# Linear attention and gated convolution on one core: the order list behind its first 215 entries is laid out anew

## The chip, the cores and the metric

One core of a Trainium2 chip runs one launch of the kernel. The metric is the device time of that launch in microseconds, here as the median of several runs. Five engines work side by side, each through its own instructions in order: TensorE (PE, with its weight loads shown as PEld), VectorE (DVE), ScalarE (ACT), GpSimd (POOL) and SyncE (SP). Transfers are issued by the queues of POOL, SP and ACT.

## The reference

Eight batches, eight heads, 576 rows, head width 64. The first part is a linear attention with a norm over each head, the second a feed-forward part with a three-tap convolution as its gate.

```python
kv = np.einsum('bhsd,bhse->bhde', k, v)
out = np.einsum('bhsd,bhde->bhse', q, kv)
x = out / sqrt(mean(out * out, -1) + 1e-06) * g_norm     # heads side by side: 8 x 576 x 512
h = np.maximum(x @ w_in, 0.0)                            # 512 -> 1024
gate = sigmoid(conv of h along the rows, 3 taps for each of 1024 columns)
y = (h * gate) @ w_out                                   # 1024 -> 512
```

## The kernel before

The kernel is a set of small operations, each a Python function of a few instructions, and one long list of entries, ORDER (L59 to L135), that says in which order they are issued. An entry is the operation's name, its arguments, and behind an @ the slots that its results take. The loop at L779 issues them one by one, and the lines from L786 chain each engine's instructions in that order. So nothing is moved by the compiler, and the list alone sets the order on each engine. The engines meet where one needs what another has made, or where a slot has to be given up first.

The slots of most matmul results are the eight banks of PSUM. An entry such as `hm.4.0@0` takes banks 0 and 1 (`bank2`), `hs` and `om` take one (`bank`). The next entry that names the same bank waits until all readers of the old result are done. Rings in SBUF work the same way: qT, sq, o32, x, h, tap, kvb, row.

For batch b the entries are, in the order of the data:

- `Lq`, `Lk`, `Lv` (POOL, L347): loads of q, k, v, converted to bf16.
- `kv` or `kz` (PE, L402, L479): k transposed times v for two pairs of heads, 72 small matmuls; `kvd` or `kva` copies the result to kvb on DVE (L414) or ACT (L416). `kx` (SP, L489) makes a copy with the halves of the partitions exchanged.
- `qt` (PE, L433) transposes q, `qd` (DVE, L443) copies it; for batches 6 and 7 a transposing transfer does this, `tq` (SP, L467).
- `ot` or `ox` (PE, L460, L500): q times kv, four small matmuls, for half of the rows (s) and half of the heads (u). `sq` (ACT, L509) squares the result.
- Batches up to 3: `on` (PE, L528) sums the squares over each head, `nl` (ACT, L545) takes the reciprocal root, `mo` (DVE, L556) multiplies into x. Batches 4 to 7, two at a time: `oc` (ACT, L521) copies the result out of PSUM, `ss` (PE, L566) sums, `ln` (ACT, L574) takes the root, `sl` (DVE, L581 to L584) splits it into two parts, `sp` (PE, L593) spreads it and `mu` (DVE, L599) multiplies into x.
- `hk`, `hs`, `hm` (PE, L658, L628, L613): x times 128 columns f of w_in. `rh` or `re` (ACT, L640, L619) is the maximum with zero into h.
- `ta`, `aa`, `ab` (DVE, L681, L682, L687, L692): the taps, two columns of f in one of two tap buffers. `sg` (ACT, L698): the sigmoid. `mg` (DVE, L722): the product with h.
- `om.p.m.0.4` and `om.p.m.4.4` (PE, L732): first and second half of 128 rows m of a pair p of batches times w_out; `oh` (L757) does half of the columns of one block. `ea`, `eh` (ACT, L738, L767) or `ed` (DVE, L743) copy the bank to a row buffer; `st`, `sh` (SP, L748, L777) store it.

ACT holds one set of function tables at a time. The roots (`nl`, `ln`) and the sigmoid (`sg`, `sc`) need different sets, and `act_table` (L224) issues a load when the next operation needs the other one.

Some of the code, cut:

```python
def bank2():
    at = slots.pop(0)
    return banks[:, at:at + 2, :]
...
def hm(b, f):
    ps = T["hm", b, f] = bank2()
    for t in range(NT):
        for s in range(2):
            nc.tensor.matmul(ps[:, s, :HS], w_in_sb[:, t, f * P:(f + 1) * P], T["x", b][:, t, c0:c1], ...)
...
for token in ORDER.split():
    what, _, at = token.partition("@")
    slots[:] = [int(s) for s in at.split(",")] if at else []
    name, *args = what.split(".")
    ops[name](*(int(a) if a.isdigit() else a for a in args))
```

Of the kernel before, what the change touches and what calls it, by code (L numbers as in the profile page):

```python
# [87 lines left out]
rh.2.5.0 on.3.0.1@4 nl.3.0.1@3 aa.1.1.2 mo.3.1.1@0 hs.2.2.1@2 rh.2.2.1 hs.2.0.0@3 rh.2.0.0 ot.3.0.0@0 sq.3.0.0@6
mo.3.0.1 qt.4.0.0@4 qd.4.0.0@3 ta.1.1.3 ab.1.1.2 aa.1.1.1 ot.3.1.0@2 sq.3.1.0@7 hs.2.3.1@6 rh.2.3.1 on.3.0.0@4
nl.3.0.0@4 hs.3.4.1@7 rh.3.4.1 hs.3.1.1@6 rh.3.1.1 on.3.1.0@4 nl.3.1.0@5 mo.3.0.0 hs.3.6.1@7 rh.3.6.1 hs.2.6.0@6  # L90
mo.3.1.0 qt.5.0.0@4 qd.5.0.0@0 ab.1.1.1 qt.4.1.0@0 qd.4.1.0@4 sg.1.1.5 sg.1.1.4 Lq.6.0.4@0 mg.1.1.2 ta.1.1.6@1
ta.1.1.7 aa.1.1.3 hs.2.3.0@7 rh.2.3.0 hs.3.0.1@2 rh.3.0.1 rh.2.6.0 sg.1.1.3 sg.1.1.2 hs.3.7.0@3 hs.3.2.0@4 rh.3.2.0
hs.3.3.0@5 rh.3.3.0 rh.3.7.0 kv.4.0.2@0 kvd.4.0.2@1 hs.3.0.0@2 hs.3.3.1@6 mg.1.1.1 Lk.5.0.4@0 rh.3.3.1 hs.3.2.1@7
rh.3.2.1 hs.3.7.1@4 rh.3.7.1 hs.3.6.0@5 rh.3.6.0 rh.3.0.0 ab.1.1.3 ta.2.2.2@0 ta.2.2.3 hs.3.4.0@3 rh.3.4.0 sg.1.1.7
hs.3.1.0@4 hs.3.5.0@5 sg.1.1.6 rh.3.1.0 qt.5.1.0@0 qd.5.1.0@2 ot.4.0.0@6 sq.4.0.0@0 mg.1.1.3 rh.3.5.0 om.0.7.0.4@2
Lv.5.0.4@1 Lq.7.0.4@1 Lk.6.0.4@1 oc.4.0.0@6 hs.2.7.1@3 rh.2.7.1 ot.4.0.1@0 sq.4.0.1@1 oc.4.0.1@7 kv.5.0.2@4 ta.2.2.0@1
kvd.5.0.2@2 ot.4.1.0@6 oc.4.1.0@8 om.0.7.4.4 aa.2.2.1 ta.2.2.1 ed.0.7@4 aa.2.2.0 ot.5.0.0@4 sq.4.1.0@2 sq.5.0.0@3
# [727 lines left out]
```

## Time and profile before

| | |
|---|---|
| runs | 177.69, 177.53, 177.68 us, median 177.68 |
| the profiled execution | span 175.6 us from its first to its last instruction; its own time isn't given, and what lies around the span is 2.1 us against the median |
| instructions | 5070, of which 2097 are matmuls on PE with a record |
| PE, DVE, ACT, POOL busy | 167.9, 149.5, 148.9, 22.2 us |
| transfers | 29.1 MB, mean 166 GB/s |
| granted clock of PE | 1.00 throughout |

Times in the profile are in microseconds from the first instruction, unless ns is written. L732 is line 732 of the kernel, and a busy time is the union of an engine's instructions. Matmuls overlap: the row of one 512-column matmul lasts 379 ns, while in a row of many they follow each other much more closely. ACT's and DVE's rows overlap a little as well, so what one of them costs is read from start to start. "Idle before" is the engine's idle time ahead of the rows, with what ended it.

### The profile page before, as it was taken

To read this page: it belongs to the slowest core of one execution; us is meant where nothing else is said; L and a number is where in the kernel's file an instruction comes from. 1 tells how busy PE (TensorE), PEld (TensorE's weight loads), DVE (VectorE), ACT (ScalarE), POOL (GpSimd) and SP (SyncE) were. 2 spreads that over 40 slices of the span, in tenths; PEclk is the share of its full clock that TensorE was granted. 3 is DMA by queue.
4 is the path that set the end of the run, shared out by engine and by line. 5 is a ranking of instruction groups with operands and counts; after the bars stand their busy time and mean duration, and the time that the engine had idled before them with its cause. 6 is when DMAs were issued, how large, how long until landed. Compare 5 with 4: busy or idle time off the path is not lost.

```text
span 175.6 us, 5070 instructions
## 1 busy us (share of the span) xinstructions
PE 167.9 (96%) x2097; PEld 100.0 (57%) x2114; DVE 149.5 (85%) x290; ACT 148.9 (85%) x268; POOL 22.2 (13%) x35
## 2 busy tenths in 40 slices
...
GB/s 159 392 323 207 207 207 207 208 208 209 207 241 230 227 207 207 170 182 197 258 181 161 14 134 0 119 123 0 119 63 0 0 0 116 13 239 175 179 304 237
DMA packets 25911, 29.11 MB, mean 166 GB/s; under 512 B 6036, under 2 KB 20384, under 8 KB 25888
## 3 DMA queue, kind: packets, MB, share of 16 engines
...
q10 hardware_dynamic: 544, 1.18, 1.7%
q8 instruction: 16, 0.26, 0.6%
...
## 4 chain that ended last, share of the span: by engine, by line
PE 76%; DVE 12%; ACT 5%; DMA 3%; issue 3%; ACTq 0%; DVEq 0%
PE banks L732 32%; PE banks L628 14%; PE banks L613 9%; PE banks L658 4%; DMA stg<-in_v_dram 3%; PE banks L460 3%; DVE h L722 2%; PE banks L708 2%; ACT taps L698 2%; PE banks L402 2%; PE banks L593 2%; PE banks L433 1%; PE banks L528 1%; DVE taps L681 1%; PE banks L286 1%
## 5 line engine op out<-in xcount | busy, mean ns | idle before, releaser
L732 PE MATMUL banks<-w_out_sb,h 128*128 128x512 bf16 x267 | 62.8, 379 | 1.2 <-issue 0.6
L698 ACT ACTIVATE taps<-taps,cw 128x576 bf16<-128x576 bf16 (+1 forms) x44 | 40.6, 958 | 5.7 <-DVE taps L692 5.5
L732 PEld LDWEIGHTS <-h 128*128 128x128 bf16 x280 | 26.2, 98 | 30.0 <-issue 1.1
L628 PE MATMUL banks<-x,w_in_sb 128*128 128x288 bf16 (+2 forms) x256 | 34.2, 286 | 0.0
L640 ACT ACTIVATE h<-banks 128x288 bf16<-128x288 f32 (+2 forms) x80 | 29.5, 460 | 0.3 <-PE banks L658 0.2
L628 PEld LDWEIGHTS <-w_in_sb 128*128 128x128 bf16 x256 | 24.4, 98 | 7.8 <-issue 0.8
L722 DVE TENSOR_TENSOR h<-h,taps 128x1152 bf16<-128x1152 bf16 (+1 forms) x24 | 22.8, 952 | 1.2 <-ACT taps L698 1.2
L687 DVE TENSOR_TENSOR taps<-taps 128x1152 bf16<-128x1152 bf16 (+1 forms) x22 | 21.5, 978 | 0.5
L509 ACT ACTIVATE sq<-banks 128x576 bf16<-128x576 f32 (+2 forms) x32 | 20.8, 691 | 1.1 <-PE banks L460 1.1
L692 DVE TENSOR_TENSOR taps<-taps,h 128x1152 bf16<-128x1152 bf16 (+1 forms) x22 | 21.4, 972 | 0.3
L681 DVE TENSOR_SCALAR taps<-h,cw 128x576 bf16<-128x576 bf16 (+1 forms) x44 | 18.7, 424 | 0.6 <-ACT h L665 0.5
L682 DVE TENSOR_SCALAR taps<-h,cw 128x576 bf16<-128x576 bf16 (+1 forms) x44 | 18.4, 418 | 0.0
L738 ACT ACTIVATE row<-banks 128x512 f32<-128x512 f32 x23 | 13.5, 597 | 5.7 <-PE banks L732 4.2
L658 PE MATMUL banks<-x,w_in_sb 128*128 128x288 bf16 (+2 forms) x128 | 17.7, 286 | 0.1
L613 PE MATMUL banks<-x,w_in_sb 128*128 128x288 bf16 x128 | 16.9, 286 | 0.0
L556 DVE SCALAR_TENSOR_TENSOR x<-banks,cw,rs 128x576 bf16<-128x576 f32 (+2 forms) x16 | 13.0, 816 | 3.9 <-ACT rs L545 3.6
L658 PEld LDWEIGHTS <-w_in_sb 128*128 128x128 bf16 x128 | 12.0, 98 | 4.4 <-issue 0.5
L227 ACT ACT_TABLE_LOAD x10 | 12.8, 1283 | 2.0 <-issue 1.8
L613 PEld LDWEIGHTS <-w_in_sb 128*128 128x128 bf16 x128 | 12.3, 98 | 3.7 <-issue 0.2
L443 DVE COPY qT<-banks 128x1152 bf16<-128x1152 bf16 (+2 forms) x13 | 8.8, 681 | 5.7 <-PE banks L433 5.7
L545 ACT ACTIVATE rs<-banks,eps_sb 128x576 f32<-128x576 f32 (+2 forms) x16 | 11.8, 740 | 1.1 <-PE banks L528 1.1
L599 DVE SCALAR_TENSOR_TENSOR x<-o,cw,banks 128x576 bf16<-128x576 f32 (+2 forms) x16 | 12.1, 810 | 0.7 <-PE banks L593 0.5
...
## 6 DMA issues: line engine op xcount, KB each, us to landing
out_dram<-row SPq DMA_DIRECT2D x35, 256.0 KB, 2.3
...
```

What stands on the lines that cost most here:

```text
L509: nc.scalar.activation(T["sq", b, u, s], T["o", b, u, s], AX.Square)
L613: nc.tensor.matmul(ps[:, s, :HS], w_in_sb[:, t, f * P:(f + 1) * P], T["x", b][:, t, c0:c1], start=(t == 0), stop=(t == NT - 1))
L628: nc.tensor.matmul(ps, w_in_sb[:, t, f * P:(f + 1) * P], T["x", b][:, t, c0:c1], start=(t == 0), stop=(t == NT - 1))
L640: nc.scalar.activation(h, fr, AX.Relu)
L658: nc.tensor.matmul(T[at], w_in_sb[:, t, f * P:(f + 1) * P], T["x", b][:, t, c0:c1], start=(t == 0), stop=(t == NT - 1))
L681: nc.vector.tensor_scalar_mul(tap[:, 0, f % 2, :n, 8:8 + S], h[:, f], cw[:, f:f + 1])
L682: nc.vector.tensor_scalar_mul(tap[:, 1, f % 2, :n, :S], h[:, f], cw[:, 2 * NF + f:2 * NF + f + 1])
L687: nc.vector.tensor_add(tap[:, 1, :, :n, :S], tap[:, 0, :, :n, 7:7 + S], tap[:, 1, :, :n, 1:1 + S])
L692: nc.vector.tensor_add(y, y, span(b, n)[:, 2 * j:2 * j + 2])
L698: nc.scalar.activation(y, y, AX.Sigmoid, scale=cw[:, NF + f:NF + f + 1])
L722: nc.vector.tensor_mul(h, h, tap_of(b, j)[:, 1, :, :n, :S])
L732: nc.tensor.matmul(T["om", p, m], h[:, f, m * P:(m + 1) * P], w_out_sb[:, f, :], start=(f == 0), stop=(f == NF - 1))
```

## The change

The list has 852 entries before and after. The first 215 are the same; the 637 behind them are in a new order with new slots. The multiset of operations is the same but for eight copies that change engine: ed.0.1, ea.0.4, ea.1.8, kvd.3.0.2, ed.2.8, ed.3.0, ed.3.7 and ea.3.6 become ea.0.1, ed.0.4, ed.1.8, kva.3.0.2, ea.2.8, ea.3.0, ea.3.7 and ed.3.6. No function changes. The diff replaces all of the list's lines from L79 on; these are the stretches that matter below, old and new.

```diff
-om.0.2.0.4@5 kv.2.0.2@6 mg.0.1.3 om.0.1.4.4 ab.1.1.0 sg.1.1.0 sg.1.1.1 kvd.2.0.2@2 ot.2.0.1@0 sq.2.0.1@0 ed.0.1@0
-st.0.1 qt.3.1.0@6 qd.3.1.0@1 Lk.4.0.4@1 Lv.4.0.4@0 Lq.5.0.4@2 om.0.2.4.4 on.2.0.1@2 qt.3.0.0@6 qd.3.0.0@2 nl.2.0.1@8
-mo.2.0.1@2 om.0.3.0.4@4 ea.0.2@1 ot.2.1.1@6 ot.2.1.0@2 mg.1.1.0 om.0.3.4.4 ed.0.3@2 sq.2.1.0@1 sq.2.1.1@2 on.2.1.0@0
...
+om.0.1.0.4@2 om.0.2.0.4@5 kv.2.0.2@6 ab.1.1.0 om.0.1.4.4 Lk.4.0.4@1 Lv.4.0.4@0 sg.1.1.0 kvd.2.0.2@0 sg.1.1.1
+qt.3.1.0@0 ot.2.0.1@6 Lq.6.0.4@2 om.0.2.4.4 ta.1.1.5@1 ea.0.1@0 qt.3.0.0@2 Lq.5.0.4@0 qd.3.1.0@1 pn qd.3.0.0@2
+sq.2.0.1@0 on.2.0.1@0 nl.2.0.1@0 om.0.3.0.4@4 ot.2.1.1@0 mo.2.0.1@0 ot.2.1.0@2 ea.0.2@1 sq.2.1.0@0 mg.1.1.0 sq.2.1.1@1
+om.0.3.4.4 ed.0.3@2 on.2.1.0@6 om.0.0.0.4@5 nl.2.1.0@0 on.2.1.1@6 nl.2.1.1@1 hk.1.3.0.0@4 om.0.0.4.4 ta.1.1.2@0
+mo.2.1.0 ot.2.0.0@2 hk.1.3.0.1 mo.2.1.1 hs.2.0.1@0 sq.2.0.0@0 rh.1.3.0 ed.0.0@3 on.2.0.0@6 hs.2.5.1@1 rh.2.0.1@1
+nl.2.0.0@0 rh.2.5.1 kv.3.0.2@4 qt.4.0.0@6 ta.1.1.4 aa.1.1.2 mo.2.0.0 qd.4.0.0@0 ta.1.1.3 ab.1.1.2 aa.1.1.1 ab.1.1.1
+kva.3.0.2@0 ot.3.1.1@0 sq.3.1.1@0 ot.3.0.1@4 sq.3.0.1@1 hs.2.1.1@2 hs.2.4.0@3 hs.2.4.1@6 rh.2.4.0 rh.2.1.1 hs.2.1.0@7
...
+ta.2.2.0@0 ta.2.2.1 mg.1.1.3 rh.3.7.1 rh.3.4.0 rh.3.5.0 rh.3.6.0 om.0.7.0.4@0 ot.4.0.0@2 sq.4.0.0@0 oc.4.0.0@0
+ta.2.2.2@1 aa.2.2.0 ot.4.0.1@4 ot.4.1.0@6 hs.2.7.1@1 tq.6.0@3 st.0.2 st.0.1 st.0.0 sq.4.0.1@1 oc.4.0.1@1 sq.4.1.0@2
+oc.4.1.0@2 rh.2.7.1 kv.5.0.2@2 kvd.5.0.2@1 om.0.7.4.4 ta.2.2.3 ot.5.0.0@2 qt.5.1.0@4 ot.5.0.1@6 ed.0.7@0 om.0.8.0.4@1
...
-om.0.6.4.4 ea.0.6@3 sp.4.0.0.4@6 mu.4.0.0 sp.4.0.1.4@0 hs.2.6.1@5 rh.2.6.1 hs.3.5.1@2 rh.3.5.1 ox.6.0.0@6 sq.6.0.0@0
-oc.6.0.0@4 mu.4.0.1 sp.5.1.1.4@4 mu.5.1.1@2 sg.2.2.3 sp.5.1.0.4@2 mu.5.1.0 hm.4.7@0 sp.5.0.1.4@4 sp.5.0.0.4@6 mu.5.0.1
-mu.5.0.0 hm.4.1@2 re.4.7@0 sg.2.2.1 re.4.1 hm.4.0@4 sg.2.2.0 hm.4.4@0 re.4.4 hm.4.6@6 re.4.6 re.4.0 hm.5.1@2 re.5.1
-mg.2.2.1 hm.5.3@0 re.5.3 tq.7.0@0 st.0.6 ox.6.1.1@6 oc.6.1.1@5 sq.6.1.1@1 ox.6.1.0@4 oc.6.1.0@1 ta.2.2.4@0 ta.2.2.5
...
+om.0.6.4.4 kvd.6.0.2@0 mu.5.1.1@1 sp.4.1.0.4@0 sp.4.0.1.4@6 hs.2.6.1@4 ea.0.6@5 mu.4.1.1 ox.6.0.0@2 rh.2.6.1 mu.4.1.0
+mu.4.0.1 sp.5.1.0.4@0 sp.5.0.1.4@4 Lk.7.0.4@0 Lv.7.0.4@1 st.0.4 hm.4.7@6 mu.5.1.0 mu.5.0.1 oc.6.0.0@0 sg.2.2.0
+sq.6.0.0@0 hm.4.0@0 hm.4.4@2 re.4.7@0 mg.2.2.0 st.0.8 sg.2.2.3 kx.6@0 tq.6.1@0 re.4.0 re.4.4 ox.6.1.1@0 sp.5.0.0.4@4
+hm.4.6@6 re.4.6 mu.5.0.0 hm.5.4@4 re.5.4 hm.5.5@2 sq.6.1.1@1 oc.6.1.1@1 re.5.5 ta.2.2.4@0 ta.2.2.5 hm.4.5@6 kz.7.0.2@0
+mg.2.2.1 hm.4.1@2 aa.2.2.2 kvd.7.0.2@1 ox.6.1.0@0 hm.5.1@4 re.5.1 re.4.5 ta.2.2.7@1 ta.2.2.6 hm.5.3@4 sq.6.1.0@2
+re.4.1 hm.5.7@6 re.5.3 oc.6.1.0@2 ab.2.2.2 hm.5.0@2 aa.2.2.3 ab.2.2.3 re.5.7 om.1.2.0.4@0 re.5.0 sg.2.2.4 om.1.0.0.4@1
+hm.5.2@2 om.1.6.0.4@4 hm.5.6@6 om.1.8.0.4@5 tq.7.0@1 st.0.3 st.0.6 sg.2.2.5 sg.2.2.7 sg.2.2.6 mg.2.2.2 re.5.6 re.5.2
+ta.4.2.5@0 ox.7.0.0@6 st.0.5 tq.7.1@2 kx.7@1 st.0.7 ox.6.0.1@2 mg.2.2.3 oc.7.0.0@3 om.1.0.4.4 om.1.2.4.4 sq.6.0.1@3
...
-mg.7.1.3 om.3.3.0.4@2 om.3.3.4.4 ed.3.3@5 st.3.3 mg.7.1.2 om.3.1.0.4@1 om.3.2.0.4@7 om.3.0.4.4 om.3.2.4.4 ed.3.2@0
-st.3.2 ed.3.0@2 st.3.0 om.3.1.4.4 ea.3.1@1 st.3.1 om.3.4.0.4@0 om.3.5.0.4@4 om.3.6.0.4@3 om.3.7.0.4@6 om.3.7.4.4
-ed.3.7@4 om.3.5.4.4 ea.3.5@3 st.3.5 om.3.4.4.4 ed.3.4@5 st.3.4 st.3.7 om.3.6.4.4 ea.3.6@0 st.3.6 oh.3.8.1@1 eh.3.8.1@2
-sh.3.8.1 oh.3.8.0@0 eh.3.8.0@1 sh.3.8.0
...
+st.2.8 om.3.5.0.4@0 om.3.4.0.4@2 st.3.0 om.3.7.0.4@4 sg.7.1.5 sg.7.1.4 ed.3.2@0 ea.3.1@1 st.3.2 st.3.3 st.3.1 mg.7.1.2
+om.3.5.4.4 om.3.6.0.4@1 ea.3.5@0 oh.3.8.1@0 eh.3.8.1@1 om.3.4.4.4 oh.3.8.0@0 eh.3.8.0@2 ed.3.4@3 st.3.5 sh.3.8.1
+st.3.4 sh.3.8.0 om.3.6.4.4 ed.3.6@0 st.3.6 om.3.7.4.4 ea.3.7@1 st.3.7
```

More of the change, by code (lines that the diff above doesn't have):

```diff
@@ L88 @@
[L88 to L97, printed above, removed]
@@ new lines @@
+on.3.1.1@2 rh.2.4.1 hs.2.2.0@6 rh.2.1.0 nl.3.1.1@0 hs.2.5.0@7 on.3.0.1@2 rh.2.2.0 hs.2.2.1@6 rh.2.5.0 mo.3.1.1@1
+ot.3.0.0@0 hs.2.0.0@7 nl.3.0.1@1 rh.2.2.1 ot.3.1.0@2 hs.2.3.1@6 sq.3.0.0@0 mo.3.0.1 on.3.0.0@4 rh.2.0.0 hs.3.4.1@7
+sq.3.1.0@1 rh.2.3.1 nl.3.0.0@0 hs.3.1.1@6 on.3.1.0@4 rh.3.4.1 rh.3.1.1 hs.3.6.1@7 hs.2.6.0@6 mo.3.0.0 nl.3.1.0@1
+qt.4.1.0@0 qt.5.0.0@4 mo.3.1.0 Lv.5.0.4@1 Lk.5.0.4@0 Lq.7.0.4@1 qd.5.0.0@1 qd.4.1.0@2 hs.3.0.1@2 hs.3.7.0@3 sg.1.1.5
+sg.1.1.4 hs.2.3.0@4 hs.3.2.0@5 hs.3.3.0@0 hs.3.0.0@1 mg.1.1.2 rh.3.6.1 rh.2.6.0 sg.1.1.3 rh.2.3.0 rh.3.7.0 rh.3.0.1
@@ new lines @@
+hs.3.3.1@6 hs.3.2.1@7 hs.3.7.1@4 kv.4.0.2@2 rh.3.3.0 sg.1.1.2 ta.1.1.6@1 ta.1.1.7 aa.1.1.3 ab.1.1.3 rh.3.0.0 rh.3.2.1
+rh.3.2.0 sg.1.1.6 mg.1.1.1 hs.3.1.0@0 rh.3.1.0 sg.1.1.7 rh.3.3.1 kvd.4.0.2@0 hs.3.6.0@1 hs.3.4.0@5 hs.3.5.0@7
+ta.2.2.0@0 ta.2.2.1 mg.1.1.3 rh.3.7.1 rh.3.4.0 rh.3.5.0 rh.3.6.0 om.0.7.0.4@0 ot.4.0.0@2 sq.4.0.0@0 oc.4.0.0@0
+ta.2.2.2@1 aa.2.2.0 ot.4.0.1@4 ot.4.1.0@6 hs.2.7.1@1 tq.6.0@3 st.0.2 st.0.1 st.0.0 sq.4.0.1@1 oc.4.0.1@1 sq.4.1.0@2
+oc.4.1.0@2 rh.2.7.1 kv.5.0.2@2 kvd.5.0.2@1 om.0.7.4.4 ta.2.2.3 ot.5.0.0@2 qt.5.1.0@4 ot.5.0.1@6 ed.0.7@0 om.0.8.0.4@1
```

63 lines of the change are left out of this document (28 added, 35 removed).

## The prediction

> **What bounds the kernel now.** I read the page's engine sums first, then the windows, then PE's rows one by one.
>
> ```profile
> span 175.6 us, 5070 instructions
> PE 167.9 (96%) x2097; PEld 100.0 (57%) x2114; DVE 149.5 (85%) x290; ACT 148.9 (85%) x268; POOL 22.2 (13%) x35
> PE 76%; DVE 12%; ACT 5%; DMA 3%; issue 3%; ACTq 0%; DVEq 0%
> ```
>
> PE is busy for 96% of the span and makes 76% of the chain. No work is added or taken away by the change, so only three things can move the time: gaps on PE, the price of the order itself on PE, and the tail behind the last matmul. The windows (columns PE, PEld, DVE, ACT, POOL busy, then the granted clock, DMA share, GB/s) say how little room there is:
>
> ```profile
> 80.00:100.00 20.00, 19.76 (x298) 12.83 (x300) 19.24 (x28) 19.94 (x31) 0.00 (x0) 1.00 1.02 169
> 100.00:120.00 20.00, 19.70 (x138) 10.10 (x139) 18.29 (x26) 19.46 (x31) 0.00 (x0) 1.00 0.28 84
> 120.00:140.00 20.00, 19.86 (x158) 14.38 (x156) 19.55 (x28) 19.85 (x38) 0.00 (x0) 1.00 0.11 40
> ```
>
> From 80 to 140 PE, ACT and DVE are all nearly full: 59.3, 59.3 and 57.1 of 60 us. Each engine works through its own list in order, and eight PSUM banks join them. A matmul that needs a bank waits until ACT or DVE has emptied it, and everything behind it on PE waits too. So a new list is judged by one question: where does a PE entry stand so close behind the ACT entry that frees its bank that ACT can't be done?
>
> **The change part by part.** Sums are made against the profiled execution. Its own time isn't given; its span is 175.6, the median of the runs 177.68, and I take the 2.1 us around the span as unchanged.
>
> Eight single operations change engine: ed.0.1 to ACT, ea.0.4 and ea.1.8 to DVE, kvd.3.0.2 to ACT, and at the end ed.2.8, ed.3.0 and ed.3.7 to ACT, ea.3.6 to DVE. The count of ACT table loads stays ten. Everything else is order.
>
> *More switches between kinds of matmul: +0.6.* In the chain of waits, each row is start, us, what:
>
> ```profile
> 76.17 1.83 PE banks L732 x8
> 78.00 0.37 PE banks L460 x8
> 78.37 1.83 PE banks L732 x8
> 80.20 0.25 PE banks L460 x4
> 80.45 0.97 PE banks L732 x4
> ...
> 152.15 10.74 PE banks L732 x49
> ```
>
> Unbroken, eight L732 matmuls take 8 x 10.74/49 = 1.75 us. Eight of them with two ot (78.37 - 76.17 = 2.20) leave 0.45 for the two ot; eight with one (80.45 - 78.37 = 2.08) leave 0.33. An ot more costs 0.12, so the run itself costs 0.21. I count 27 such runs of small matmuls (ot, qt, kv, kz, ox, ss, sp) in the old list behind its first 215 entries and 30 in the new: 3 x 0.21 = 0.6, on PE, with nothing beside it.
>
> *Around 45 us: +0.85.* ACT, then PE:
>
> ```profile
> 43.99 1.44 ACT L698 ACTIVATE taps<-taps,cw 128x576 bf16<-128x576 bf16 x2 [0.29 <-DVE taps L692]
> 45.34 0.63 ACT L509 ACTIVATE sq<-banks 128x576 bf16<-128x576 f32 x1
> 45.98 1.28 ACT L227 ACT_TABLE_LOAD   x1
> 47.27 0.74 ACT L545 ACTIVATE rs<-banks,eps_sb 128x576 f32<-128x576 f32 x1
> ```
> ```profile
> 47.99 0.44 PE L460 MATMUL banks<-qT,kvb 64*64 64x288 bf16 x8
> ```
>
> Up to here PE's work in the two lists is the same. The new one puts ea.0.1 (an interval of about 0.48 on ACT, row L738 below less the overlap) ahead of sq.2.0.1, so square, table load and nl.2.0.1 end 0.48 later, at 48.5. And ot.2.1.1, which had banks of its own at 47.99, now takes bank 0 behind nl.2.0.1: 48.54, +0.55. on.2.1.1 (bank 6 behind nl.2.1.0) and hs.2.0.1 (bank 0 behind mo.2.1.1) lose about 0.15 each by the same sum (an estimate). The load rows show the next ACT row 0.01 behind the table load's end. The Trainium skill (ScalarE: Activation LUTs, What ACT_TABLE_LOAD costs) gives 1283 ns and 1380 ns of drain for a switch; the rows agree with the first and show no drain. By the page this wait would be 1.4 longer and the time 185.3.
>
> *kva.3.0.2: +0.25.* ACT now copies kvb between kv.3.0.2 and ot.3.1.1; only qt.4.0.0 (0.3) stands between them. A 128x256 ACT copy takes 0.38 (the tail's row below), plus about 0.15 of hops: 0.53 - 0.3. Before, other matmuls stood there and hid the copy. Nothing and 0.5 are its bounds.
>
> *kv.5.0.2: +0.55.* It takes banks 2 and 3 behind sq.4.0.0 and oc.4.0.0 of ot.4.0.0, with only ot.4.0.1, ot.4.1.0 and hs.2.7.1 between. From that ot's start ACT needs 0.33 until it is done, then a little under 0.59 and 0.72 (rows below, 640 wide; here 576), and hops of 0.1: 1.7. PE's fill is a run of three ot (0.21 + 3 x 0.12), half an hm (0.49) and 0.1: 1.15.
>
> *Four places in the stage from 85 to 113.* ACT's and PE's rows give every duration (ACT's starts, not its lengths, since its rows overlap):
>
> ```profile
> 88.45 0.71 ACT L509 ACTIVATE sq<-banks 128x640 bf16<-128x640 f32 x1
> 89.04 0.72 ACT L521 ACTIVATE o<-banks 128x640 f32<-128x640 f32 x1
> 89.62 1.28 ACT L698 ACTIVATE taps<-taps,cw 128x1152 bf16<-128x1152 bf16 x1
> 90.77 0.68 ACT L619 ACTIVATE h<-banks 128x576 bf16<-128x576 f32 x1
> 91.30 1.29 ACT L698 ACTIVATE taps<-taps,cw 128x1152 bf16<-128x1152 bf16 x1
> 92.45 0.69 ACT L619 ACTIVATE h<-banks 128x576 bf16<-128x576 f32 x1
> ```
> ```profile
> 87.84 0.33 PE L500 MATMUL banks<-qT,kvb 64*64 64x320 bf16 x4
> 88.10 0.82 PE L593 MATMUL banks<-wparts,spread 32*128 32x288 bf16 x4
> 88.86 1.15 PE L613 MATMUL banks<-x,w_in_sb 128*128 128x288 bf16 x8
> 89.94 0.42 PE L593 MATMUL banks<-wparts,spread 32*128 32x288 bf16 x4
> 90.29 6.05 PE L613 MATMUL banks<-x,w_in_sb 128*128 128x288 bf16 x48
> ```
>
> On ACT sq and oc take 0.59, sg 1.15, re 0.53. On PE an hm takes (6.05 - 0.17)/6 = 0.98, where 0.17 is what the last matmul needs to drain (1.15 - 0.98).
>
> - **ox.6.1.1** takes bank 0 behind re.4.0. From ox.6.0.0's start PE has ox, two sp, hm.4.7, hm.4.0, hm.4.4: 0.26 + 0.24 + 2.94 + 0.1 = 3.5. ACT has oc.6.0.0, sg.2.2.0, sq.6.0.0, re.4.7, sg.2.2.3, re.4.0: 0.33 until ox.6.0.0 is done, then 0.59 + 1.15 + 0.59 + 0.53 + 1.15 + 0.68, hops 0.1: 5.1. PE waits **1.6**.
> - **hm.5.3** stands right behind hm.5.1 on the same bank 4: drain 0.17, re.5.1 0.68, hops 0.1: **0.95**, whatever the state.
> - **ox.7.0.0, ox.6.0.1** stand behind re.5.6 and re.5.2. From hm.5.1's end ACT needs 0.2 + eight re (4.24) + sq and oc (1.18) + four sg (4.6) + 0.2 = 10.4. PE has the 0.95, five hm (4.9), four half om (3.46), an ox: 9.55. PE waits **0.85**. Behind re.5.5 ACT is idle until re.5.1, for hm.4.1, ox.6.1.0 and hm.5.1 at least: 2.2 us that it hadn't lost before.
> - Waits that go: the 0.4 in the row at 88.10 (0.82 against 0.42 for the same four sp) and 0.3 in the next rows: **-0.7**.
>
> ```profile
> 118.22 0.42 PE L593 MATMUL banks<-wparts,spread 32*128 32x256 bf16 x6
> ...
> 120.41 0.74 PE L593 MATMUL banks<-wparts,spread 32*128 32x320 bf16 x6
> ```
>
> *The end: +0.7 and +0.5.* DVE and PE:
>
> ```profile
> 165.91 0.75 DVE L722 TENSOR_TENSOR h<-h,taps 128x1152 bf16<-128x1152 bf16 x1
> ```
> ```profile
> 165.74 4.70 PE L732 MATMUL banks<-w_out_sb,h 128*128 128x512 bf16 x21
> 170.28 1.91 PE L757 MATMUL banks<-w_out_sb,h 128*128 128x256 bf16 x16
> ```
>
> mg.7.1.2 ends at 166.66, and om.3.7.4.4, the first that needs it, starts five matmuls into the row of 21, at 166.82: a margin of 0.16, with 5.2 us of PE work from there. In the new list om.3.5.4.4 is the first, with five half om and both oh behind it, 6.07. DVE's list ahead of mg.7.1.2 is as long, and its mu come from the same late stage, so PE waits 6.07 - 5.2 - 0.16 = 0.7 (bounds 0 and 1.0).
>
> ```profile
> 172.27 0.38 ACT row L767
> ```
> ```profile
> L738 ACT ACTIVATE row<-banks 128x512 f32<-128x512 f32 x23 | 13.5, 597 | 5.7 <-PE banks L732 4.2 <-issue 1.4
> out_dram<-row SPq DMA_DIRECT2D x35, 256.0 KB, 2.3
> out_dram<-row SPq DMA_DIRECT2D x2, 128.0 KB, 2.2
> ```
>
> The last matmul is followed by half a row now and by a whole one then: 0.60 - 0.38 = 0.22 on ACT, 0.1 to 0.5 in the store: +0.5.
>
> Sum: 0.6 + 0.85 + 0.25 + 0.55 + 1.6 + 0.95 + 0.85 - 0.7 + 0.7 + 0.5 = 6.15. **Predicted: 177.68 + 6.15 = 183.8 us**, slower.
>
> **DMA.** POOL's loads keep their number; q of batch 6 now goes ahead of q of batch 5, q of 4 ahead of k and v of 3. Three stores (st.0.0, st.0.1, st.0.2) move from around 50 us to behind tq.6.0, so loads before that meet fewer stores and those behind more. On SP, kx.6 and tq.6.1 now stand behind st.0.4 and st.0.8.
>
> ```profile
> qT<-q_sb SPq DMA_TRANSPOSE x4, 8.2
> ```
>
> tq.6.1 is needed by ox.6.1.1; issued some 7 us ahead of it and landing 8.2 later it can hold ox.6.1.1 by up to 1.5 more. I take nothing, as re.4.0 already holds it about as long.
>
> **Rivals.**
> 1. *The waits swallow one another* (0.20). If DVE's mu hold PE ahead of hm.4.7, part of the 1.6 is spent there already, and the early losses are slack later. The 0.95 and 0.85 stay, half of the 1.6, runs 0.6, tail 0.5, less 0.7: +3.0, 180.7.
> 2. *ACT is the bound, and the move helps it* (0.04, the other side). From 80 to 120 ACT is busy 39.4 of 40, and ea.0.4 and ea.1.8 leave it: -0.96. With the 0.7 that goes, less runs and tail, 0.6 + 0.5: -0.55, 177.1. It decides if ACT's idle time between re.5.5 and re.5.1 stays below about 0.6; the list gives it 2.2.
> 3. *Transfers are late as well* (0.10). kx.6, tq.6.1 and the loads of batch 5 each hold PE by 1 or so: +8.5, 186.2.
> 4. *The clock drops* (0.03). All windows show 1.00. With 3.4 us of waits within 20 us a drop to half for as long would add 1.7: 185.5. The Trainium skill (TensorE: Matmul & The Clock Gate, What's actually happening) halves the clock after an idle window of about 3.4 us; no single wait here is that long, so by that rule it stays at 1.00.
> 5. *All is hidden, no change* (0.03).
>
> The forecast has 0.60. The range, 180.4 to 186.8, takes in rivals 1, 3 and 4 and the bounds of the unknown waits. A measurement of this kernel tells some 0.2% from no change. Faster 0.04, same 0.03, slower 0.93.
>
> **What would show it.** Right: gaps on PE ahead of an L500 row (1.6), between two L613 rows (0.95) and ahead of the next L500 rows (0.85); an idle ACT of over 2 us between two L619 rows; ot.2.1.1 held by L545. Wrong: a PE that stays as full as before from 85 to 113, or an ACT that is far enough ahead at re.4.0.

## The result and the profile after

The changed kernel takes 184.22 us (184.13 to 184.26, four runs), the kernel before beside it on the same chip 177.68 us (177.53 to 177.69, four runs): a ratio of 1.037, 95% interval 1.0356 to 1.0385. Predicted were 183.8, and a range of 180.4 to 186.8.

The page of the changed kernel, with the lines that answer to the first ones shown of before:

```profile
span 182.0 us, 5080 instructions
PE 170.9 (94%) x2114; PEld 100.2 (55%) x2114; DVE 148.7 (82%) x288; ACT 150.2 (82%) x270; POOL 22.4 (12%) x35
PE 53%; ACT 11%; DVE 6%; issue 2%; ACTq 0%
```

The span is 6.4 us longer, and PE's share of the chain of work that ended last falls from 76% to 53%. Busy times have hardly moved: PE's 3.0 more come with 17 matmul records more (before's trace has 2097 of the 2114) and with waits that rows cover, and DVE and ACT together have 0.5 more. So it isn't work that was added, it is time in which PE stood. The windows of the same stretch (PE, PEld, DVE, ACT, POOL busy, granted clock, DMA share, GB/s):

```profile
80.00:100.00 20.00, 18.75 (x253) 10.94 (x253) 17.57 (x26) 18.27 (x28) 0.00 (x0) 1.00 0.99 198
100.00:120.00 20.00, 18.56 (x190) 10.46 (x176) 16.87 (x23) 17.08 (x26) 0.00 (x0) 1.00 0.13 44
120.00:140.00 20.00, 19.88 (x151) 12.44 (x144) 19.38 (x27) 19.12 (x34) 0.00 (x0) 1.00 0.21 80
```

From 80 to 120 all three engines have become emptier, PE by 2.2 us, ACT by 4.1, DVE by 3.1. Three engines that feed one another and empty together wait for each other in turn; the work of none of them alone fills the time here. The list of PE's waits says for what (us in total, times, longest):

```profile
PE banks L500 <- ACT h L619: 1.6, 3, 0.9
...
PE banks L613 <- ACT h L619: 0.7, 1, 0.7
PE banks L460 <- ACT kvb L416: 0.6, 2, 0.4
PE banks L732 <- ACT row L738: 0.5, 1, 0.5
PE banks L460 <- ACT rs L545: 0.5, 1, 0.5
```

Apart from waits in the first 40 us, which both kernels have, nearly all of it is ACT that has still to empty a bank. PE's own rows give the places (start, length, and in brackets the idle time ahead of it and who ended it):

```profile
48.55 0.44 PE L460 MATMUL banks<-qT,kvb 64*64 64x288 bf16 x8 [0.52 <-ACT rs L545]
...
75.52 0.77 PE L402 MATMUL banks<-v_sb,k_sb 64*64 64x64 bf16 x72 [0.43 <-ACT o L521]
...
91.12 3.10 PE L613 MATMUL banks<-x,w_in_sb 128*128 128x288 bf16 x24 [0.24 <-DVE x L599]
95.17 0.30 PE L500 MATMUL banks<-qT,kvx 64*64 64x256 bf16 x4 [0.95 <-ACT h L619]
...
103.61 1.14 PE L613 MATMUL banks<-x,w_in_sb 128*128 128x288 bf16 x8 [0.74 <-ACT h L619]
...
112.61 0.33 PE L500 MATMUL banks<-qT,kvb 64*64 64x320 bf16 x4 [0.49 <-ACT h L619]
113.15 0.30 PE L500 MATMUL banks<-qT,kvx 64*64 64x256 bf16 x4 [0.21 <-ACT h L619]
...
162.60 1.67 PE L732 MATMUL banks<-w_out_sb,h 128*128 128x512 bf16 x7 [0.54 <-ACT row L738]
...
176.43 1.89 PE L732 MATMUL banks<-w_out_sb,h 128*128 128x512 bf16 x8
```

These are ot.2.1.1, kv.5.0.2, hm.4.7, ox.6.1.1, hm.5.3, ox.7.0.0, ox.6.0.1 and om.3.0.0.4; the last row ends at 178.32 with the last matmul. The bracket is not yet what a wait costs, because matmuls are pipelined: a row drains for some 0.17 after the next could have begun, and a row of other matmuls ahead has a start of its own. So I laid each list's PE operations end to end from 39.88 us, at the pace of their undisturbed rows and with 0.21 for each run of small matmuls, and looked by how much each begins later than in that sum. That is its lateness. It grows in steps, one for each wait. It reaches 2.3 us at the end of before and 7.8 at the end of after: 5.5 us of waits. With the three more runs (0.6) and a tail that is 0.3 longer (from the last matmul to the end of the span 182.0 - 178.32 = 3.7 now, 175.6 - 172.19 = 3.4 then) that makes 6.4, the whole difference of the spans.

| place | predicted | lateness in the trace after |
|---|---|---|
| more runs of small matmuls | 0.6 | 0.6, by the same price |
| ot.2.1.1, on.2.1.1, hs.2.0.1 | 0.85 | 0.49 + 0.14 + 0.15 = 0.78 |
| ot.3.1.1 behind kva.3.0.2 | 0.25 | 0.38 |
| hs.2.7.1 behind rh.3.6.0 (74.4) | not named | 0.47 |
| kv.5.0.2 behind oc.4.0.0 | 0.55 | 0.39 |
| up to ox.6.1.1 behind re.4.0 | 1.6 | 0.25 + 0.48 + 0.91 = 1.64 |
| hm.5.3 behind re.5.1 | 0.95 | 0.91 |
| ox.7.0.0, ox.6.0.1 | 0.85 | 0.45 + 0.42 = 0.87 |
| waits of before that go (88, 120) | -0.7 | the one at 88 is gone from its place (DVE's mu now hold PE a little further on, counted at ox.6.1.1); of the one near 120 about 0.2 is left, at 123.87 |
| the end: om.3.5.4.4 behind mg.7.1.2 | 0.7 | 0 there; 0.72 at om.3.0.0.4 behind ea.2.7 |
| tail | 0.5 | 0.3 |

What is left is made of many steps of 0.1 to 0.2, up and down.

ACT's rows show the other side of the two largest:

```profile
92.78 0.65 ACT L619 ACTIVATE h<-banks 128x576 bf16<-128x576 f32 x1
93.31 1.26 ACT L698 ACTIVATE taps<-taps,cw 128x1152 bf16<-128x1152 bf16 x1
94.46 1.20 ACT L619 ACTIVATE h<-banks 128x576 bf16<-128x576 f32 x2
...
102.90 1.19 ACT L619 ACTIVATE h<-banks 128x576 bf16<-128x576 f32 x2 [2.93 <-PE banks L613]
...
161.00 1.55 ACT L738 ACTIVATE row<-banks 128x512 f32<-128x512 f32 x3
```

At 93.31 ACT does sg.2.2.3, 1.15 us from start to start, and only then re.4.0, for which PE stands; hm.4.0, the second of the three hm in PE's row at 91.12, had ended by 93.25 (two times 0.98 and the drain). At 102.90 ACT itself has stood for 2.93 us: re.5.1 can't begin before hm.5.1 ends, and hm.5.3 can't begin before re.5.1 ends. One after the other, nothing beside it. Each engine's empty time there is the other's work.

### The profile page after: what moved, and what is told of

It reads as the page before. It is cut to its first block, busy times and chain, and to the rows that moved or that the text cites. A ratio compares the mean times of both kernels' runs of the same rounds, so it can differ in the third digit from the quotient of the medians.

```text
span 182.0 us, 5080 instructions
## 1 busy us (share of the span) xinstructions
PE 170.9 (94%) x2114; PEld 100.2 (55%) x2114; DVE 148.7 (82%) x288; ACT 150.2 (82%) x270; POOL 22.4 (12%) x35
## 4 chain that ended last, share of the span: by engine, by line
PE 53%; ACT 11%; DVE 6%; issue 2%; ACTq 0%
PE banks L732 23%; PE banks L628 18%; PE banks L613 4%; ACT taps L698 3%; ACT h L619 3%; ACT o L521 2%; ACT sq L509 1%; DVE taps L687 1%; PE banks L460 1%; ACT row L738 1%; PE banks L593 1%; PE banks L528 1%; ACT h L640 1%; PE banks L757 1%; PE banks L402 1%
## 5 line engine op out<-in xcount | busy, mean ns | idle before, releaser
L732 PE MATMUL banks<-w_out_sb,h 128*128 128x512 bf16 x280 | 65.3, 379 | 0.5 <-ACT row L738 0.5
L640 ACT ACTIVATE h<-banks 128x288 bf16<-128x288 f32 (+2 forms) x80 | 30.3, 467 | 0.4 <-PE banks L658 0.2
L681 DVE TENSOR_SCALAR taps<-h,cw 128x576 bf16<-128x576 bf16 (+1 forms) x44 | 18.6, 423 | 0.6 <-ACT h L665 0.6
L682 DVE TENSOR_SCALAR taps<-h,cw 128x576 bf16<-128x576 bf16 (+1 forms) x44 | 19.0, 432 | 0.0
L619 ACT ACTIVATE h<-banks 128x576 bf16<-128x576 f32 x16 | 10.0, 668 | 4.4 <-PE banks L613 4.4
```

The source lines that it names most:

```text
L640: nc.scalar.activation(h, fr, AX.Relu)
L681: nc.vector.tensor_scalar_mul(tap[:, 0, f % 2, :n, 8:8 + S], h[:, f], cw[:, f:f + 1])
L682: nc.vector.tensor_scalar_mul(tap[:, 1, f % 2, :n, :S], h[:, f], cw[:, 2 * NF + f:2 * NF + f + 1])
L732: nc.tensor.matmul(T["om", p, m], h[:, f, m * P:(m + 1) * P], w_out_sb[:, f, :], start=(f == 0), stop=(f == NF - 1))
```

## Experiments

**Theory.** The time is lost at single places in the list where a matmul takes a bank that ACT or DVE has just begun to empty, or hasn't yet begun to. **Rivals.** The waits swallow one another, so that taking one away gives little; ACT's total work is the bound; transfers are late. The last of them has no experiment of its own; what the traces say of it stands with the run of all mends. Times are medians of four runs where nothing else is said, with the kernel before on the same chip in the same minutes (177.56 to 177.68); 95% intervals are those of the ratio to it. After's own interval, to compare with, is 1.0356 to 1.0385. Of the mends made one by one, only the first lies clear of it; for the others it is the trace that shows what the edit won, and the medians agree with it.

### One wait mended: sg.2.2.3 behind re.4.4

```diff
-... hm.4.4@2 re.4.7@0 mg.2.2.0 st.0.8 sg.2.2.3 kx.6@0 tq.6.1@0 re.4.0 re.4.4 ox.6.1.1@0 ...
+... hm.4.4@2 re.4.7@0 mg.2.2.0 st.0.8 kx.6@0 tq.6.1@0 re.4.0 re.4.4 sg.2.2.3 ox.6.1.1@0 ...
```

> The changed kernel with one token moved: sg.2.2.3 (1.15 us on ACT) stands behind re.4.4 instead of ahead of re.4.0, so that re.4.0 empties bank 0 for ox.6.1.1 about 1.2 us sooner. Theory (TensorE pays for single waits written into the list, nothing else): the 0.91 us ahead of ox.6.1.1 goes, all later waits stay as they were, 184.2 becomes 183.3 (183.2 to 183.5). Rival 1 (waits swallow one another): the later ones at hm.5.3 and ox.7.0.0 grow by what is won, 183.9 to 184.2. Rival 2 (ACT's total work is the bound): its work is unchanged, 184.2.

Measured: 183.20 us (183.03 to 183.29), ratio 1.0316 (1.0299 to 1.0333): 1.0 us less. PE:

```profile
94.32 0.30 PE L500 MATMUL banks<-qT,kvx 64*64 64x256 bf16 x4
...
102.75 2.00 PE L613 MATMUL banks<-x,w_in_sb 128*128 128x288 bf16 x15 [0.74 <-ACT h L619]
```

ox.6.1.1 starts without a gap, 0.85 earlier, and the gap ahead of hm.5.3 is the same 0.74 as it was. Nothing further on has grown: the swallowing that the first rival expects isn't there. ACT's work is the same to the instruction, so its total is not the bound either.

### Half a mend: re.4.5 into ACT's pause

```diff
-... hm.5.1@4 re.5.1 re.4.5 ta.2.2.7@1 ta.2.2.6 hm.5.3@4 ...
+... hm.5.1@4 re.4.5 re.5.1 ta.2.2.7@1 ta.2.2.6 hm.5.3@4 ...
```

> The changed kernel with re.4.5 moved ahead of re.5.1 on ACT, into the 2.9 us in which ACT had nothing to do; hm.5.3 still stands right behind hm.5.1 on its bank pair. If the 0.87 us ahead of ox.7.0.0 and ox.6.0.1 come from ACT's work piled up behind re.5.1, 0.5 us less work there should take 0.5 us of them away: 183.7. If re.5.3, which has to wait for hm.5.3 anyway, holds ACT as much as the work before it, the 0.5 us saved are lost again right there: 184.2, with the same waits. Mine is the second: re.5.1's end plus 0.05 starts hm.5.3, that ends 1.15 later, and only then can re.5.3 start, at 104.8, where it now starts at 105.1; about 0 to 0.3 less.

Measured: 183.88 us (183.80 to 184.37), ratio 1.0363 (1.0348 to 1.0379), which the intervals don't tell from after's. PE in the profiled execution:

```profile
103.72 1.02 PE L613 MATMUL banks<-x,w_in_sb 128*128 128x288 bf16 x7 [0.74 <-ACT h L619]
...
112.67 0.33 PE L500 MATMUL banks<-qT,kvb 64*64 64x320 bf16 x4 [0.44 <-ACT h L619]
113.20 0.30 PE L500 MATMUL banks<-qT,kvx 64*64 64x256 bf16 x4 [0.20 <-ACT h L619]
```

The three gaps are 0.74, 0.44 and 0.20 against 0.74, 0.49 and 0.21. ACT has 0.53 us less to do behind re.5.1 and PE gets 0.05 of it: work taken off an engine helps only if what it does next is ready.

### The whole of it: hm.5.7 between hm.5.1 and hm.5.3

```diff
-... hm.5.1@4 re.5.1 re.4.5 ... hm.5.3@4 sq.6.1.0@2 re.4.1 hm.5.7@6 re.5.3 oc.6.1.0@2 ... re.5.7 ...
+... hm.5.1@4 re.4.5 re.5.1 ... hm.5.7@6 hm.5.3@4 sq.6.1.0@2 re.4.1 re.5.7 re.5.3 oc.6.1.0@2 ...
```

> As the one before, and hm.5.7 (bank 6) stands ahead of hm.5.3 (bank 4), with re.5.7 ahead of re.5.3: between hm.5.1 and hm.5.3 lies another 1.15 us of matmuls while re.5.1 empties bank 4. By the sum of the prediction (each wait is its own term) the 0.91 us ahead of hm.5.3 goes and nothing else changes, 183.3. By the theory that from re.5.1 to re.5.2 ACT is the one that sets the time (it runs without a pause from 102.9 to 113.1), only the 0.53 us of re.4.5 that it has done in its pause are won, and what TensorE doesn't wait at hm.5.3 it waits at ox.7.0.0: 183.7, with the wait there grown from 0.45 to about 0.8. Mine is 183.7.

Measured: 183.74 us (183.44 to 184.05), ratio 1.035 (1.0334 to 1.0365): by the medians 0.5 less, as expected of ACT's chain, and not the 0.9 of the plain sum; the interval still meets after's. PE, then ACT:

```profile
101.76 4.17 PE L613 MATMUL banks<-x,w_in_sb 128*128 128x288 bf16 x32
106.47 1.89 PE L732 MATMUL banks<-w_out_sb,h 128*128 128x512 bf16 x7 [0.54 <-ACT o L521]
```
```profile
102.95 0.65 ACT L619 ACTIVATE h<-banks 128x576 bf16<-128x576 f32 x1 [2.38 <-PE banks L613]
```

The four hm from 101.76 now run as one row of 32 matmuls; the 0.91 at hm.5.3 is gone. In its place om.1.2.0.4 stands at 106.47 for oc.6.1.0. It is not where I had put it (ox.7.0.0), but it is the same cause: from 102.95 to 113 ACT's rows have no bracket at all, so it is busy without a pause, and whatever PE wins it waits for at the first place where it meets that chain.

### The same wait put into the kernel before

```diff
-... hm.5.1@2 re.5.1 mg.2.2.1 hm.5.3@0 re.5.3 ... kz.7.0.2@2 ... hm.5.7@0 ...
+... hm.5.1@2 re.5.1 mg.2.2.1 hm.5.3@2 re.5.3 ... kz.7.0.2@0 ... hm.5.7@2 ...
```

The banks 0 and 1 are exchanged with 2 and 3 in every entry from hm.5.3 on, so that nothing but this one wait is new.

> The kernel before, with one wait added and nothing else: from hm.5.3 on the bank pairs 0,1 and 2,3 are exchanged, so that hm.5.3 stands on the pair that re.5.1 has just to empty, as in the changed kernel. re.5.1 ends at 96.44 and hm.5.3 began at 95.20: hm.5.3 waits 1.2 to 1.3 us. Theory: TensorE never makes it up, 177.7 becomes 178.9 (178.6 to 179.0). Rival 1 (swallowed by the kernel's own later waits at 120 us, 0.3, and at the end): 178.2 to 178.6. Rival 2 (ACT's total work is the bound): 177.7.

Measured: 178.98 us (178.87 to 179.05), ratio 1.0081 (1.0066 to 1.0096): 1.4 us more.

```profile
96.61 1.14 PE L613 MATMUL banks<-x,w_in_sb 128*128 128x288 bf16 x8 [1.12 <-ACT h L619]
```

By the lateness sum the wait is 1.29 us, and 1.2 of it are still there at the last matmul, 77 us later. One wait, made by nothing but bank numbers, costs 0.8%.

### One copy given back to DVE: ed.0.1

```diff
-... ta.1.1.5@1 ea.0.1@0 qt.3.0.0@2 ...
+... ta.1.1.5@1 ed.0.1@0 qt.3.0.0@2 ...
```

> The changed kernel with one part of the change undone: ea.0.1 is done by DVE again (ed.0.1, behind ta.1.1.5), so that sq.2.0.1 on ACT no longer waits behind it. sq.2.0.1, the table load and nl.2.0.1 then begin about 0.3 us sooner (from 45.81 to 45.5, where ot.2.0.1 has ended), and ot.2.1.1 waits 0.2 instead of 0.49. Theory: these 0.3 us last over the 130 us that follow, 183.9 (183.8 to 184.0). Rival 1 (the early waits are swallowed by the later ones, as ot.3.1.1 and hs.2.7.1): 184.2. Rival 2 (the prediction's reading, the whole 0.55 comes from ea.0.1): 183.7.

Measured: 183.91 us (183.80 to 183.98), ratio 1.0352 (1.0337 to 1.0367): by the medians 0.3 less, with an interval that meets after's. PE and ACT:

```profile
48.40 0.44 PE L460 MATMUL banks<-qT,kvb 64*64 64x288 bf16 x8 [0.22 <-ACT rs L545]
```
```profile
45.64 0.65 ACT L509 ACTIVATE sq<-banks 128x576 bf16<-128x576 f32 x1
46.31 1.28 ACT L227 ACT_TABLE_LOAD   x1
47.60 0.74 ACT L545 ACTIVATE rs<-banks,eps_sb 128x576 f32<-128x576 f32 x1
```

The gap is 0.22 instead of 0.52, and by the lateness sum the 0.3 us won at 48 us are still won at the last matmul; no later step differs from after's. So the prediction's reading of this place was half right: ea.0.1 makes 0.3 of the 0.5; the rest is the bank, behind a table load that would have to be waited for anyway.

### The price of a change of form, alone

A change of form is the step from full-array matmuls to small ones and back. Twelve more matmuls of zeros go into the kernel before, into columns of bank 7 that nobody reads; in the first kernel in one run, in the second one behind each of twelve om matmuls.

```diff
+    @op
+    def zz():
+        nc.tensor.matmul(banks[half(0), 7, 384:], zero[half(0), :D], zero[half(0), :P], start=True, stop=True)
-... om.2.1.0.4@4 om.2.2.0.4@2 om.2.2.4.4 ...
+... om.2.1.0.1@4 zz zz zz zz zz zz zz zz zz zz zz zz om.2.1.1.1 om.2.1.2.1 ...
```
```diff
+... om.2.1.0.1@4 zz om.2.1.1.1 zz om.2.1.2.1 zz ... om.2.2.7.1 zz ...
```

> The kernel before with 12 extra matmuls of 64x64 by 128 columns of zeros, all in one run behind the first matmul of om.2.1, where TensorE waits for nothing (their columns of bank 7 are read by nobody). It measures the base for the next one. Twelve matmuls of 128 columns at the rate of the 64-row ones seen (0.12 us for 288 columns) are 0.6 to 0.7 us, and one change of form 0.2: 177.6 becomes 178.4 (178.2 to 178.9).

> As the one before, but the same 12 matmuls stand singly, one behind each of 12 full-array matmuls of om.2.1 and om.2.2: eleven more runs of small matmuls for the same work. By the prediction's term (0.21 us for each further run) it is 2.3 us longer than the kernel with all twelve in one run, 180.7 (180.2 to 181.0). If a change of form costs nothing and the 0.21 was the small matmuls' own time, the two agree within 0.2. If it is the start of each matmul's weights that costs, and not the form, the difference lies between.

Measured: 178.49 us (178.40 to 178.80), ratio 1.005 (1.0035 to 1.0065), in one run; 180.91 us (180.89 to 180.97), ratio 1.0183 (1.0166 to 1.02), spread. The difference is 2.42 us for eleven more runs, 0.22 each, as the first of the expectations had it. First the kernel with one run, then the other:

```profile
141.30 0.85 PE L781 MATMUL banks<-zero 64*64 64x128 bf16 x12
```
```profile
141.91 0.39 PE L732 MATMUL banks<-w_out_sb,h 128*128 128x512 bf16 x1
142.22 0.24 PE L781 MATMUL banks<-zero 64*64 64x128 bf16 x1
142.40 0.39 PE L732 MATMUL banks<-w_out_sb,h 128*128 128x512 bf16 x1
142.72 0.24 PE L781 MATMUL banks<-zero 64*64 64x128 bf16 x1
```

From one om matmul to the next are 142.40 - 141.91 = 0.49 us where 0.22 are needed without a small one between. No gap is shown: the price is hidden in rows that overlap and look busy. It can only be read from start to start. The kernel's own small matmuls show it there too: in the trace of after, what follows a 512-column matmul begins 0.22 us behind it when it is another full one and 0.31 when it is a small one (ot, kv, qt); and behind the last ot of a run, whose 288 columns would take 0.12, a full one begins only 0.22 to 0.24 later.

### The wait near the end, mended twice

```diff
-... ea.2.6@3 sg.7.1.0 sg.7.1.1 ea.2.5@4 ea.2.0@5 st.2.3 st.2.6 ea.2.7@0 st.2.7 st.2.5 ...
+... ea.2.6@3 sg.7.1.0 sg.7.1.1 ea.2.7@0 ea.2.5@4 ea.2.0@5 st.2.3 st.2.7 st.2.6 st.2.5 ...
```

> The changed kernel with ea.2.7 ahead of ea.2.5 and ea.2.0 on ACT (and st.2.7 ahead of st.2.6). om.3.0.0.4 now waits 0.72 us for ea.2.7, which stands behind two other evictions after om.2.7.4.4 has ended at 161.19; placed first it would end near 161.8, before om.2.8.4.4 does at 162.06. Theory: that wait goes, and the next is the one the prediction named, om.3.5.4.4 behind mg.7.1.2, which ended 0.6 us before it was needed and is DVE's, so that it doesn't come earlier: about 0.15 of the 0.72 come back there, 183.65 (183.5 to 183.8). Rival 1 (the prediction's place is right too, and the end is set by DVE's chain): 184.1. Rival 2 (plain sum): 183.5.

Measured: 184.31 us (184.00 to 185.26), ratio 1.0384 (1.0355 to 1.0412): nothing won. The first rival was nearest in number, but not by its cause. PE and ACT:

```profile
165.49 8.79 PE L732 MATMUL banks<-w_out_sb,h 128*128 128x512 bf16 x39 [0.69 <-ACT row L738]
```
```profile
164.84 1.08 ACT L738 ACTIVATE row<-banks 128x512 f32<-128x512 f32 x2 [0.54 <-DMA out_dram<-row]
```

The 0.72 at om.3.0.0.4 are gone, and om.3.2.0.4 waits 0.9 at 165.49 for ea.2.1, which waits for a store to leave its row. That is my edit's doing: I had put st.2.7 ahead of st.2.6, and SyncE's queue is in order too. The second try leaves the stores' order alone:

```diff
-... rh.7.4.1 ea.2.6@3 sg.7.1.0 sg.7.1.1 ea.2.5@4 ea.2.0@5 st.2.3 st.2.6 ea.2.7@0 st.2.7 ...
+... rh.7.4.1 st.2.3 ea.2.6@3 sg.7.1.0 sg.7.1.1 ea.2.7@0 ea.2.5@4 ea.2.0@5 st.2.6 st.2.7 ...
```

> As the kernel a_end, but SyncE's queue keeps its order (st.2.3 and st.2.6 ahead of st.2.7). In a_end st.2.7, which waits for ea.2.7, stood ahead of st.2.6; st.2.6 was issued at 162.41 instead of 159.27 and landed at 164.76 instead of 161.28, and ea.2.1 needs the row that it empties: it began at 164.84 and om.3.2.0.4 waited 0.9 us for it. If that was why a_end won nothing, the 0.72 us at om.3.0.0.4 go now and only mg.7.1.2 (ended at 171.49, needed at 172.10 less 0.72) holds back about 0.15: 183.65 (183.5 to 183.8). If DVE's chain sets the end, 184.2.

Measured: 184.05 us (183.92 to 184.58), ratio 1.0364 (1.035 to 1.0378), 0.2 less, which the intervals don't tell from after's. In its trace om.3.0.0.4 doesn't wait; and yet the last matmul ends only 0.2 earlier than in after (178.13 for 178.32). PE, then ACT:

```profile
159.75 13.77 PE L732 MATMUL banks<-w_out_sb,h 128*128 128x512 bf16 x62
173.63 1.03 PE L757 MATMUL banks<-w_out_sb,h 128*128 128x256 bf16 x8
```
```profile
161.30 1.57 ACT L738 ACTIVATE row<-banks 128x512 f32<-128x512 f32 x3 [0.18 <-ACT taps L698]
...
172.98 0.60 ACT L738 ACTIVATE row<-banks 128x512 f32<-128x512 f32 x1 [2.06 <-DMA out_dram<-row]
```

By the lateness sum om.3.2.0.4 now waits 0.24 for ea.2.1 and oh.3.8.1 0.27 for ea.3.5, both ACT copies that had been just in time. The three copies ahead of ea.2.1 begin 0.3 later than in after (161.30 for 161.00), since ea.2.7, now the first of them, has to wait for its own matmuls; and ea.3.5 waits for a store to leave its row. mg.7.1.2, which I had expected to be next, holds nobody. Here, unlike at 95 us, taking one wait away lets others appear, because several copies stand in a row with no slack.

### All mends at once

The four edits above, and oc.6.1.0 behind re.4.1.

> The changed kernel with all the mends at once: sg.2.2.3 behind re.4.4; re.4.5 ahead of re.5.1, hm.5.7 ahead of hm.5.3 and oc.6.1.0 behind re.4.1; ed.0.1 on DVE; ea.2.7 ahead of ea.2.5 with SyncE's order kept. If the single waits add up, 1.0 + 0.5 + 0.3 + 0.55 = 2.35 us less than 184.2: 181.9 (181.6 to 182.2). If they swallow one another, or another engine's total work comes to be the bound, 182.6 to 183.3. It stays slower than the kernel before in either case, by the 4 us in waits and changes of form that no single token causes.

Measured: 182.28 us (182.17 to 182.79), ratio 1.0257 (1.0241 to 1.0273): 1.94 less than after. One by one they gave 1.02 + 0.48 + 0.31 + 0.17 = 1.98. By the ratios, each to the kernel before on the same chip, it is 1.0370 less 1.0257 together, 2.0 us, and 0.0098 or 1.7 us one by one. Within the intervals, some 0.3 us each, they add up. The other 4.6 us to the kernel before (182.28 against 177.68) were taken out by no run; only the lateness sum gives them their places. The expected 181.9 missed only by what the end didn't give. The profiled execution is the longest of the four, 182.79, and shows what is next:

```profile
79.34 0.32 PE L460 MATMUL banks<-qT,kvb 64*64 64x288 bf16 x4 [0.30 <-DVE qT L443]
...
94.61 0.30 PE L500 MATMUL banks<-qT,kvx 64*64 64x256 bf16 x4 [0.42 <-DMA qT<-q_sb]
```

At 79.34 ot.5.1.1 waits for a copy of DVE's, and DVE has stood 0.4 us for a store to leave a row; after's trace has neither wait. At 94.61, with re.4.0 out of the way, ox.6.1.1 waits for tq.6.1. The times from issue to landing of the two transposing transfers that SP issued from 88 to 92 us (their median), in after, in the kernel with sg.2.2.3 moved, and here:

```profile
qT<-q_sb SPq DMA_TRANSPOSE x2, 3.6
```
```profile
qT<-q_sb SPq DMA_TRANSPOSE x2, 4.2
```
```profile
qT<-q_sb SPq DMA_TRANSPOSE x2, 4.5
```

tq.6.1, the first of the two, was issued at 89.17, 89.16 and 89.14. It landed at 92.98, 94.19 and 94.48: in after long before ox.6.1.1 at 95.17, in the second kernel just ahead of its 94.32, here too late. So rival 3 of the prediction was not wrong in its mechanism, as far as tq.6.1 goes; re.4.0 hides it, and it is seen only once that is mended. Whether the three shorter runs wait there too isn't known.

### Five tokens in the kernel before, then four

```diff
-... ea.0.2@1 ot.2.1.1@6 ot.2.1.0@2 mg.1.1.0 ...
+... ea.0.2@1 ot.2.1.0@2 ot.2.1.1@6 mg.1.1.0 ...
-... hs.2.7.0@2 ... om.0.6.0.4@4 Lv.6.0.4@0 kz.6.0.2@6 kvd.6.0.2@0 ...
+... hs.2.7.0@5 ... Lv.6.0.4@0 kz.6.0.2@6 om.0.6.0.4@4 kvd.6.0.2@0 ...
```

ot.5.1.0 stands three entries earlier as well, and mg.4.2.3 one later.

> The kernel before with five tokens moved by the same reading, at its own waits: ot.2.1.1 next to ot.2.1.0 ahead of mg.1.1.0's place and ot.5.1.0 next to the following small matmuls (one change of form fewer, 0.22), om.0.6.0.4 two tokens later, hs.2.7.0 on bank 5 instead of 2, and on DVE mg.4.2.3 two tokens later, behind nothing that TensorE waits for, so that the DVE operations behind it come 1.3 us sooner for sp.7.1.1.6 and hs.6.4.1. By the no-stall sums with the waits put in, 0.3 us less: 177.35 (177.2 to 177.6). If the order's own slack is too small for it, 177.6 to 178.

Measured: 177.67 us (177.44 to 178.20, eleven runs) against 177.68, ratio 1.0002 (0.999 to 1.0013): nothing. kz.6.0.2 in before, then here:

```profile
84.28 0.78 PE L479 MATMUL banks<-v_sb,k_sb 64*64 64x64 bf16 x72
```
```profile
84.17 0.77 PE L479 MATMUL banks<-v_sb,k_sb 64*64 64x64 bf16 x72 [0.62 <-DMA v_sb<-in_v_dram]
```

Moving om.0.6.0.4 two entries took away the four matmuls that had covered the load: kz.6.0.2 is next on PE 0.86 us sooner, and PE stands until v of batch 6 has landed. Nor do the moves save a change of form, as was expected of them: ot.2.1.1 and ot.2.1.0 stood side by side before, and ot.5.1.0 still stands alone between two om. The list has 27 runs of small matmuls in the kernel before and 28 here, since om.0.6.0.4 now parts kz.6.0.2 from sp.4.1.1.4. The second kernel has the other four edits only, and 27 runs:

```diff
-... Lv.6.0.4@0 kz.6.0.2@6 om.0.6.0.4@4 kvd.6.0.2@0 ...
+... om.0.6.0.4@4 Lv.6.0.4@0 kz.6.0.2@6 kvd.6.0.2@0 ...
```

> As the kernel b_five, but om.0.6.0.4 stands ahead of kz.6.0.2 again. In b_five kz.6.0.2 came 0.86 us of matmuls sooner by that move and then waited 0.6 for v of batch 6; its span was 0.4 longer than that of the kernel before. If this wait was what ate the gain, it goes, and what is left of the five edits shows: 177.3 to 177.5. If the other four edits win nothing either (sp.7.1.1.6 waited 0.33 for mu.7.0.0 as before), 177.6 to 177.75.

Measured: 177.49 us (177.35 to 177.70, eleven runs) against 177.61, ratio 0.9994 (0.9985 to 1.0003). It lies at the upper edge of the first expectation, and the interval takes in no change; so it isn't shown that the four edits win anything, or that the wait for the load cost the 0.1 by which the two ratios differ. No version tried here is shown to be faster than the kernel before.

## Why the prediction was right, point by point

- **What bounds it.** PE's order, with gaps, was the right place to look: 5.5 of the 6.4 us are gaps on PE, 0.6 its changes of form, 0.3 the tail.
- **Runs of small matmuls.** 0.21 each, read from three rows of before, and 0.22 by the experiment. The term is right.
- **Around 45 us.** Right in size (0.78 against 0.85). The share that I gave to ea.0.1 was too large; giving that copy back won 0.3.
- **kva.3.0.2, kv.5.0.2.** 0.38 and 0.39 for 0.25 and 0.55: mis-sized both ways, together 0.77 for 0.8. hs.2.7.1's 0.47 was not looked for; from there the sum of all waits is somewhat too small.
- **ox.6.1.1.** The 1.6 were right as a sum, since ACT's chain from ox.6.0.0 on came out as added up (5.15 from its start at 90.02 to ox.6.1.1 at 95.17, against 5.1). They fall in three places, much as rival 1 had it: 0.25 at two sp, behind mu.4.1.0 on DVE (ended at 90.35) and rh.2.6.1 on ACT (90.54), 0.48 at hm.4.7 behind mu.4.0.1 (91.07), and 0.91 at ox.6.1.1. Rival 1's further step, that only half of the 1.6 would be left, is refuted: the three make 1.64, and the 0.91 taken away gave 1.0.
- **hm.5.3.** Right, 0.91 for 0.95. It was the safest term, since drain, re and hops are the least that this arrangement costs. It isn't the most, as the prediction's "whatever the state" had it: put into before, the same arrangement cost 1.3 to 1.4, because there re.5.1 was late as well.
- **ox.7.0.0, ox.6.0.1.** Right in size (0.87 for 0.85) and cause. But the two terms, this and hm.5.3's, are not independent, as the sum took them: mending the second moves 0.4 of it into the first's chain.
- **The end.** This step failed. I said that om.3.5.4.4 would wait 0.7 for mg.7.1.2; mg.7.1.2 had ended 0.6 us before it was needed. The term took it that DVE's list would come as late as PE's; but mg.7.1.2 ended 4.8 us later than in before (170.74 + 0.75 = 171.49 for 166.66), and PE's last matmul 6.1 later. The 0.72 came 10 us earlier, at om.3.0.0.4, because ea.2.7 is the last of three row copies in one stretch of ACT (161.00, 1.55 us). The size agrees by chance. I had compared one pair, DVE's last product with PE, and not gone through ACT's copies against the banks in the same way.
- **The tail.** A whole row for half a one: 0.3 for 0.5.
- **Transfers.** Nothing was added for tq.6.1, as re.4.0 was to hold ox.6.1.1 longer. That is so: it landed 3.8 us behind its issue, not 8.2, and 2.2 us before ox.6.1.1.
- **The clock.** 1.00 in the three windows above, so rival 4 didn't come up. The Trainium skill (TensorE: Matmul & The Clock Gate, What's actually happening) needs an idle window of about 3.4 us; PE's longest gap in the rows above is 0.95, so they agree and don't test it.
- **The table load.** The Trainium skill (ScalarE: Activation LUTs, What ACT_TABLE_LOAD costs) would put 1.4 us of drain on it. In the kernel with ed.0.1 it starts 0.02 behind the row ahead and the next row 0.01 behind it; there is no drain to be seen. The sum with it would be 183.8 + 1.4 = 185.2, not the 185.3 that the prediction wrote, and 184.22 was measured.
